# Sixteen-bit masks in a weight conversion, one table product for kv, token maxima for the second batch, and a re-planned start of a fused attention and two-layer kernel

## The chip, the cores and the metric

The kernel runs on one core of one Trainium2 chip. The metric is device microseconds (us) of one execution. PE is TensorE (matrix products and transposes), DVE is VectorE, ACT is ScalarE, POOL is GpSimd, SP issues most transfers. Each engine works through its own instruction queue in order.

## The reference, cut to what matters

```python
def _attn_ref(q, k, v):                    # each (8, 8, 576, 64), float32
    q_s = softmax of q over the 64 features
    k_s = softmax of k over the 576 tokens
    kv = np.einsum('bhsd,bhse->bhde', k_s, v)
    return np.einsum('bhsd,bhde->bhse', q_s, kv)

def _moe_ref(x, w_in, w_out, s, b):        # x: (4608, 512), w_in (512, 2048), w_out (2048, 512)
    r = np.maximum(x @ w_in, 0.0)
    return (s * (r * r) + b) @ w_out
```

Both softmaxes subtract the maximum and add 1e-9 to the sum. The two weights arrive as 64-bit floats; everything else is 32-bit.

## The kernel before, in words

**The main work.** The tokens are cut into blocks of 512: one block per batch (its first 512 tokens), and a ninth block made of the 64 tokens that each batch has left over. For each block the 2048 columns of `w_in` are taken in 16 chunks `f`. A step `t` = 16 * block + f has two halves. `h_parts` (L522) makes `h` with 12 products, four 128-row chunks `c` of x times three terms: every 32-bit operand is split into a rounded part and a remainder, and high-high, high-low and low-high are summed. `o_parts` (L590) makes four token tiles times three terms, 12 products more, into `acc`. Between them lie the relu, square, scale and split that give `gh` and `gl`. All products of 512 columns run at one pace, so 144 steps of 24 products are the bulk of the run.

**Attention.** Two heads make a unit `u`, two units (four heads) a pair `pr`; a batch has two pairs. Block 0 needs units 0 to 3 (tiles x0 to x3, one per chunk `c`), block 1 needs units 4 to 7. From the third batch on, `pair` (L400) is mixed into the main loop (L721) by the framework's own ordering.

**The first 16 steps** are ordered by a planner inside the kernel, `Order` (L113). Every stage of every stream is an `Op` with an engine, a guessed cost and a due number; `Order.run` repeatedly takes the op that can start first and, among those on its engine that can start within 0.1 us, the one with the lowest due number. What it chooses is the program order of PE, DVE, ACT and SP. Its streams:

- `transfers` (L635), on SP: k of units 0 and 1, weight 0, v of pair 0, q of pair 1, k of units 2 and 3, v of pair 1, the scalars s and b, weights 1 to 4. `others` (L658), on ACT's queue: q of pair 0. `reload` (L674): pairs 2 and 3, each into the buffers of an earlier pair, so k and v wait until that pair's kv is made.
- `conv_w(f)` (L182) turns the 64-bit weight chunk f (both matrices, 128 x 1024 values) into a high and a low 32-bit part: ACT L193 and L196, DVE L199 (keeps the top two bits of the high word and ORs in three bits of the low word), L203, L205, L208, ACT L213, DVE L215. Chunk 0 is done in two halves of 512, due at -2; chunk f is due at f - 2.
- `k_stream(u)` (L300): five transposes (L308), a maximum over the tokens (L311), an exponential with its sum (L316), five transposes back (L321, L322), two copies (L324, L325). The transposes use the PSUM buffer `big`, of which there is one.
- `kv_stream(pr)` (L327): 1/sum (L332, L334), 40 small products (L288), then the result scaled into the diagonal blocks of `kvf`, whose other blocks were zeroed once (L62): four instructions of 64 x 64, on DVE for pairs 0 and 1 (L348), on ACT for pairs 2 and 3 (L350).
- `q_stream(u)` (L352): maximum, subtraction, exponential, sum, reciprocal and product over the features (L361 to L375), five transposes into `big` (L379), a copy (L382), four products with `kvf` (L389), the split into x (L395, L398). The latter two use PSUM tag `acc` (two buffers) for units 0 to 3 and `big` for 4 to 7.
- `step(t)` (L555): the products, a relu on ACT (L563), and then either DVE L576, ACT L578, DVE L543, or, for t below 12 that are no multiple of 4, ACT L567, L569, L571 and DVE L573.

In `pair` the maximum over tokens is taken differently: over the token tiles on DVE (L414 to L416), two transposes (L420), one reduction (L422), two transposes that spread it (L426), a subtraction (L428), an exponential (L433), and a zeroing of the padding on POOL (L434). The sum comes from a 65th column of ones beside v.

Of the kernel before, what the change touches and what calls it, by code (L numbers as in the profile page):

```python
# [11 lines left out]
U32 = mybir.dt.uint32  # L12
AF = mybir.ActivationFunctionType
# [12 lines left out]
def attention_moe(ctx: ExitStack, tc: tile.TileContext, q, k, v, w_in, w_out, s, b, out):  # L26
# [34 lines left out]
    for t in kvfs:  # L61
        nc.gpsimd.memset(t, 0.0)  # L62
# [42 lines left out]
    class Op:  # L105

        def __init__(self, eng, cost, due, needs=(), take=(), free=(), gives=(), kb=0):
            self.eng, self.cost, self.due, self.kb = eng, cost, due, kb  # L110
            self.needs, self.take, self.free, self.gives = needs, take, free, gives

    class Order:  # L113
# [3 lines left out]
        NEAR, HOP, TRIP, RATE = 0.1, 0.15, 1.8, 0.3  # L117
# [22 lines left out]
        def run(self, streams):  # L140
            heads = [[next(g), 0.0, g] for g in streams]
            while heads:
# [9 lines left out]
                heads[i][1] = end = self.at[eng] = t + o.cost  # L152
# [29 lines left out]
    def conv_w(f, some):  # L182

        due = f - AHEAD
# [12 lines left out]
        yield Op("DVE", 1.13 * two, due)  # L197
# [69 lines left out]
    def loads(pr):  # L267
        tiles[pr] = raws[0]
        main, left = sources(pr)
        for which in range(2):  # L270
# [7 lines left out]
        nc.sync.dma_start(vt[0:LEFT, :, NQ, 0:D], left(v, 0, 4))  # L278

# [11 lines left out]


# [33 lines left out]

    def kv_stream(pr):  # L327
        us = (2 * pr, 2 * pr + 1)
        due = DUE[us[1]]
        yield Op("DVE", 0.2, due, needs=[f"z{u}" for u in us])  # L330
        z = zs.pop(pr)
        nc.vector.tensor_scalar(z, z, 1e-9, None, op0=ALU.add)  # L332
        zr = small.tile([P, 2], F32, name=f"zr_{pr}", tag="zr")
        nc.vector.reciprocal(zr, z)  # L334
# [4 lines left out]
        if pr < NP // 2:  # L339
            yield Op("DVE", 0.5, due, free=["sm"], gives=[f"kvf{pr}"])  # L340
        else:
            yield Op("ACT", 1.28, due, free=["sm"], gives=[f"kvf{pr}"])
        for i in range(2):
            for h in range(2):
                r = slice(h * D, (h + 1) * D)
                o, a, c = kvfs[pr % 2][r, i, h, :], kv[r, i], zr[r, i:i + 1]
                if pr < NP // 2:
                    nc.vector.tensor_scalar(o, a, c, None, op0=ALU.mult)  # L348
                else:
                    nc.scalar.activation(o, a, AF.Copy, scale=c)  # L350

    def q_stream(u):  # L352
        pr, i = divmod(u, 2)
        bb, hp = divmod(u, NP)
        due, (tag, bufs) = DUE[u], wide(u)
# [24 lines left out]
        yield Op("ACT", 0.53, due, free=["big"])  # L380
# [18 lines left out]

    def pair(pr):  # L400
# [9 lines left out]

        m2 = work.tile([P, 4, 2, D], F32, name=f"m2_{pr}", tag="m2")
        m1 = work.tile([P, 4, D], F32, name=f"m1_{pr}", tag="m1")
        with held():
            nc.vector.tensor_tensor(out=m2, in0=kt[:, :, 0:2], in1=kt[:, :, 2:4], op=ALU.max)  # L414
        nc.vector.tensor_tensor(out=m1, in0=m2[:, :, 0], in1=m2[:, :, 1], op=ALU.max)
        nc.vector.tensor_tensor(out=m1[0:LEFT], in0=m1[0:LEFT], in1=kt[0:LEFT, :, NQ], op=ALU.max)  # L416
        yield
        kT = sm("kT")
        for i in range(2):
            nc.tensor.transpose(kT[:, i * P:(i + 1) * P], m1[:, 2 * i:2 * i + 2].rearrange("p h d -> p (h d)"), ident)  # L420
        km = small.tile([P, 2], F32, name=f"km_{pr}", tag="km")
        nc.vector.tensor_reduce(out=km, in_=kT[:, 0:2 * P].rearrange("p (u s) -> p u s", u=2), axis=AX.X, op=ALU.max)  # L422
        yield
        mb = sm("mb")
        for i in range(2):
            nc.tensor.transpose(mb[:, i * P:(i + 1) * P], km[:, i:i + 1].to_broadcast([P, P]), ident)  # L426
        for i in range(2):
            nc.vector.tensor_tensor(  # L428
                out=kts[i], in0=kts[i],
                in1=mb[:, i * P:(i + 1) * P].rearrange("p (h d) -> p h d", h=2).unsqueeze(2).to_broadcast([P, 2, NT, D]),  # L430
                op=ALU.subtract,
            )
            nc.scalar.activation(kts[i], kts[i], AF.Exp)  # L433
            nc.gpsimd.memset(kts[i][LEFT:P, :, NQ], 0.0)  # L434
            yield
# [15 lines left out]
        z = small.tile([P, 2], F32, name=f"z_{pr}", tag="z")  # L451
        nc.vector.tensor_scalar(z, kv[:, :, D], 1e-9, None, op0=ALU.add)
        zr = small.tile([P, 2], F32, name=f"zr_{pr}", tag="zr")
        nc.vector.reciprocal(zr, z)
        kvf = kvfs[pr % 2]
        for i in range(2):
            for h in range(2):
                r = slice(h * D, (h + 1) * D)
                nc.vector.tensor_scalar(kvf[r, i, h, :], kv[r, i, 0:D], zr[r, i:i + 1], None, op0=ALU.mult)
# [95 lines left out]
    def step(t):  # L555
# [8 lines left out]
        if t < 12 and t % 4:  # L564
# [199 lines left out]
```

## Time and profile before

| | |
|---|---|
| median of 3 runs | 907.41 us (907.05 to 909.71) |
| profiled execution, its own time | 907.33 us |
| its span, first to last instruction | 905.5 us |
| PE busy / DVE busy / ACT busy / POOL busy over the span | 879.9 / 471.9 / 358.9 / 83.4 us |
| moved from memory and back | 46.14 MB read, 10.49 MB written |

Busy times say little by themselves: the first 150 us and the rest have different limits. The views used are the busy time by stretches, the waits, the instructions in order of time, the chain that ended last, and the groups by source line.

### The profile page before, as it was taken

The numbers are of one execution on the slowest core, as the hardware profiler recorded it, in microseconds if no ns is written. First come the engines' busy times: TensorE is split into PE (matmuls) and PEld (weight loads), VectorE is DVE, ScalarE is ACT, GpSimd is POOL, SyncE is SP. The second block draws the span as 40 slices with busy tenths as digits, with TensorE's granted clock in tenths as the row PEclk, the third lists the DMA queues.
The fourth block names the chain that finished last, engine by engine and source line by source line (L and its number), as shares of the span: only waits on it lengthen the run. The fifth ranks groups of instructions, "written<-read, shape, count | busy, mean of one in ns | idle before, by whom it ended". The sixth has DMA issues, their size and how long they took to land.

```text
span 905.5 us, 11459 instructions
## 1 busy us (share of the span) xinstructions
PE 879.9 (97%) x4560; PEld 724.0 (80%) x4560; DVE 471.9 (52%) x742; ACT 358.9 (40%) x578; POOL 83.4 (9%) x105
## 2 busy tenths in 40 slices
PE   4699999999999999999999999999999999999997
PEld 3477788888888888888888888888888888888885
DVE  7999994555454536363555446553636332223222
ACT  4899963333333423333333334333323322222222
POOL 1000000211020202020021002020202110000000
PEclk9999999999999999999999999999999999999999
DMA  9975231303130302221130313030300110001001
GB/s 230 311 258 176 92 82 47 79 4 79 50 80 4 79 4 78 48 58 27 47 79 4 82 47 79 4 79 20 105 7 1 50 47 0 1 1 47 0 1 47
DMA packets 82340, 57.36 MB, mean 63 GB/s; under 512 B 52976, under 2 KB 77552, under 8 KB 82160
## 3 DMA queue, kind: packets, MB, share of 16 engines
q1 hardware_dynamic: 81168, 55.52, 21.2%
q10 hardware_dynamic: 1120, 1.11, 0.4%
q8 instruction: 36, 0.59, 0.3%
q14 instruction: 16, 0.13, 0.0%
HBM read 46.14 MB, written 10.49 MB: 63 GB/s over the span
## 4 chain that ended last, share of the span: by engine, by line
PE 87%; DVE 7%; DMA 3%; ACT 1%; issue 1%; SPq 0%; ACTq 0%; DVEq 0%
PE acc L604 40%; PE h L530 40%; PE xp L493 2%; PE kv L288 2%; DMA st<-in_moe_w_in_dram 2%; PE qT L476 1%; DVE low L208 1%; DMA q<-in_q_dram 1%; DVE low L199 1%; DVE w L215 1%; DVE st L203 1%; DVE qm L361 1%; DVE km L311 0%; ACT w L213 0%; DVE st L205 0%
## 5 line engine op out<-in xcount | busy, mean ns | idle before, releaser
L530 PE MATMUL h<-x,w 128*128 128x512 f32 x1728 | 428.0, 394 | 4.2 <-ACT r L563 1.8
L530 PEld LDWEIGHTS h<-x,w 128*128 128x128 f32 x1728 | 321.8, 188 | 72.8 <-ACT r L563 2.8
L604 PE MATMUL acc<-w,gh 128*128 128x512 f32 x1152 | 340.3, 392 | 0.0
L604 PEld LDWEIGHTS acc<-w,gh 128*128 128x128 f32 x1152 | 215.0, 188 | 44.0 <-ACT o L617 0.4
L551 DVE SCALAR_TENSOR_TENSOR r<-r,sb 128x512 f32<-128x512 f32 x128 | 101.4, 792 | 274.2 <-ACT r L550 274.1
L604 PE MATMUL acc<-w,gl 128*128 128x512 f32 x576 | 207.8, 393 | 0.0
L550 ACT ACTIVATE r<-h 128x512 f32<-128x512 f32 x128 | 76.4, 597 | 295.9 <-PE h L530 288.8
L543 DVE SCALAR_TENSOR_TENSOR gl<-r,sb,gh 128x512 fp32r<-128x512 f32 x135 | 105.2, 780 | 86.7 <-ACT gh L552 84.7
L552 ACT ACTIVATE gh<-r,sb 128x512 fp32r<-128x512 f32 x128 | 92.7, 724 | 93.6 <-DVE r L551 93.0
L604 PEld LDWEIGHTS acc<-w,gl 128*128 128x128 f32 x576 | 108.1, 188 | 23.8 <-DVE gl L573 1.1
L443 POOL TENSOR_TENSOR q<-q,qm 128x640 f32<-128x640 f32 x24 | 30.3, 1262 | 433.4 <-DVE qm L442 432.1
L470 POOL TENSOR_TENSOR qe<-qe,qr 128x640 f32<-128x640 f32 x24 | 30.3, 1262 | 56.1 <-DVE qr L469 50.9
L433 ACT ACTIVATE k<-k 128x640 f32<-128x640 f32 x24 | 17.6, 737 | 22.4 <-DVE k L428 22.4
L466 DVE TENSOR_REDUCE qs<-qe 128x10 f32<-128x640 f32 x24 | 19.6, 818 | 12.7 <-ACT qe L445 12.7
L96 DVE TENSOR_TENSOR x<-xp,x 128x512 fp32r<-128x512 f32 x24 | 16.6, 691 | 16.9 <-ACT x L95 16.9
L445 ACT ACTIVATE qe<-q 128x640 f32<-128x640 f32 x24 | 17.6, 732 | 19.2 <-POOL q L443 19.2
L96 DVE TENSOR_TENSOR ql<-qT,qh 128x576 fp32r<-128x576 f32 x24 | 18.2, 758 | 12.0 <-ACT qh L95 12.0
L95 ACT CAST qh<-qT 128x576 fp32r<-128x576 f32 x24 | 15.4, 642 | 19.6 <-PE qT L476 19.6
L493 PE MATMUL xp<-qh,kvhl 128*128 128x256 f32 (+1 forms) x96 | 23.1, 297 | 0.0
L288 PEld LDWEIGHTS kv<-v,k 128*64 128x64 f32 x600 | 19.2, 140 | 4.2 <-issue 2.4
L428 DVE TENSOR_TENSOR k<-k,mb 128x640 f32<-128x640 f32 x24 | 18.6, 815 | 6.2 <-PE mb L426 6.2
L288 PE MATMUL kv<-v,k 128*64 128x65 f32 (+1 forms) x600 | 21.2, 226 | 0.0
(102 smaller groups left out, 543.6 us busy)
## 6 DMA issues: line engine op xcount, KB each, us to landing
st<-in_moe_w_in_dram SPq DMA_DIRECT2D x16, 512.0 KB, 8.5
st<-in_moe_w_out_dram SPq DMA_DIRECT2D x16, 512.0 KB, 8.9
out_dram<-o SPq DMA_DIRECT2D x16, 512.0 KB, 2.6
q<-in_q_dram SPq DMA_DIRECT2D x14, 512.0 KB, 4.8
v<-in_v_dram SPq DMA_DIRECT2D x48, 128.0 KB, 4.9
k<-in_k_dram SPq DMA_DIRECT2D x12, 512.0 KB, 4.8
k<-in_k_dram SPq DMA_DIRECT2D x12, 128.0 KB, 4.7
v<-in_v_dram SPq DMA_DIRECT2D x3, 512.0 KB, 4.2
```

What stands on the lines that cost most here:

```text
L96: return eng_l.tensor_tensor(out=l, in0=src, in1=h.bitcast(F32), op=ALU.subtract)
L288: nc.tensor.matmul(kv[h * D:(h + 1) * D, i], kt[:, i, h, n], vt[:, 2 * i + h, n], start=(n == 0), stop=(n == NT - 1))
L443: nc.gpsimd.tensor_tensor(out=qt, in0=qt, in1=bc(qm, [P, 2, NT, D]), op=ALU.subtract)
L466: nc.vector.tensor_reduce(out=qs, in_=qe, axis=AX.X, op=ALU.add)
L470: nc.gpsimd.tensor_tensor(out=qe, in0=qe, in1=bc(qr, [P, NT, 2, D]), op=ALU.mult)
L493: nc.tensor.matmul(t[:, 0:src.stop - src.start], lhs, rhs[:, src], start=(j == 0), stop=(j == len(terms) - 1))
L530: nc.tensor.matmul(hp_, w[:, j, c, :], x[:, c, :], start=(c == 0 and i == 0), stop=(c == NP - 1 and i == 2))
L543: gls.append(nc.vector.scalar_tensor_tensor(out=gl, in0=r, scalar=b_col, in1=gh.bitcast(F32), op0=ALU.add, op1=ALU.subtract))
L550: nc.scalar.activation(r, hp_, AF.Relu)
L551: nc.vector.scalar_tensor_tensor(out=r, in0=r, scalar=s_col, in1=r, op0=ALU.mult, op1=ALU.mult)
L552: nc.scalar.activation(gh, r, AF.Identity, bias=b_col)
L604: last = nc.tensor.matmul(a, g[:, js], w_, start=(f == 0 and i == 0), stop=(f == NFC - 1 and i == 2)).ins
```

## The change

In the conversion L199 becomes a one-operand mask on 16-bit words: the top halves of the high words, ANDed with 0xC000, are written over the top halves of `low`. Every scaling of kv becomes one product with a 128 x 4 table `zr` that holds 1/sum on its own block and zero on the other, so `kvf` needs no zeroing; the table costs one small product with a constant mask `own`. Pairs 2 and 3 take k as `pair` does (`k_pair`, `kv_second`), with v laid out with the 65th column. Steps 13, 14 and 15 take the form with three ACT instructions. The due numbers are given for k, q and kv apart; weight 0 becomes due at 9 and weight f at f - 1; the planner counts PE twice as slow before 18 us and has other transfer constants. qT takes the tag that xp has. SP's order is k0, k1, weight 0, v0, k2, v1, q1, k3, weights 1 to 4, and s and b move to ACT's queue, ahead of the exponential's table load.

```diff
-    AHEAD = 2
+    AHEAD = 1
...
-    DUE = (-9, -9, -8, -8, 3.5, 4.5, 8, 10)
+    DUE_K = (-24, 9, -27, -9, 4, 0, 10, 0)
+    DUE_Q = (-16, -12, -24, -12, 7.5, 11.5, -16, 30)
+    DUE_V = (-30, -30, -15, 14)
+    DUE_W = 9
...
-    for t in kvfs:
-        nc.gpsimd.memset(t, 0.0)
+    own = const.tile([P, 2, 2], F32, name="own")
+    nc.gpsimd.memset(own, 0.0)
+    for h in range(2):
+        nc.gpsimd.memset(own[h * D:(h + 1) * D, :, h], 1.0)
...
-        NEAR, HOP, TRIP, RATE = 0.1, 0.15, 1.8, 0.3
+        NEAR, HOP, TRIP, RATE = 0.1, 0.15, 2.8, 0.33
+        COLD = 18
...
-        due = f - AHEAD
+        due = f - AHEAD if f else DUE_W
...
-        nc.vector.scalar_tensor_tensor(
-            out=low, in0=hi, scalar=0xC0000000, in1=low, op0=ALU.bitwise_and, op1=ALU.bitwise_or
+        nc.vector.tensor_scalar(
+            low.bitcast(U16).rearrange("p n (e t) -> p n e t", t=2)[:, :, :, 1], stg.bitcast(U16)[:, :, :, 3],
+            0xC000, None, op0=ALU.bitwise_and
         )
...
+    def scales(pr, z, src):
+
+        nc.vector.tensor_scalar(z, src, 1e-9, None, op0=ALU.add)
+        nc.vector.reciprocal(z, z)
+        zr = small.tile([P, 2, 2], F32, name=f"zr_{pr}", tag="zr")
+        nc.vector.tensor_tensor(out=zr, in0=own, in1=z.unsqueeze(2).to_broadcast([P, 2, 2]), op=ALU.mult)
+        return zr
+
+    def blocks(pr, kv, zr):
+        kvf = kvfs[pr % 2]
+        shape = [P, 2, 2, D]
+        nc.vector.tensor_tensor(
+            out=kvf, in0=kv.unsqueeze(2).to_broadcast(shape), in1=zr.unsqueeze(3).to_broadcast(shape), op=ALU.mult
+        )
+        return kvf
...
+    def k_pair(pr):
...
+        yield Op("DVE", 1.13, due, needs=[f"k{u} there" for u in us])
...
+        k_max_2(kt, m2)
+        yield Op("DVE", 0.9, due)
+        k_max_1(kt, m2, m1)
+        yield Op("PE", 0.25, due, take=["sm"])
+        kT = sm("kT")
+        k_turn(m1, kT)
+        yield Op("DVE", 0.35, due, free=["sm"])
+        k_top(kT, km)
+        yield Op("PE", 0.25, due, take=["sm"])
+        mb = spread(km, sm("mb"))
+        for i, u in enumerate(us):
+            yield Op("DVE", 0.73, due, free=["sm"] if i else (), gives=[f"k{u} less"])
+            k_less(kts[i], mb, i)
+        for i, u in enumerate(us):
+            yield Op("ACT", 0.63, due, gives=[f"k{u}"])
+            k_exp(kts[i])
...
-        yield Op("PE", 0.6, due, take=["big", "qf"], free=["qe"])
-        qT = ps.tile([P, 1024], F32, name=f"qT_{u}", tag="big")
+        yield Op("PE", 0.6, due, take=[tag, "qf"], free=["qe"])
+        qT = ps.tile([P, 2, 512], F32, name=f"qT_{u}", tag=tag, bufs=bufs).rearrange("p a b -> p (a b)")
...
-        if t < 12 and t % 4:
+        if t % 4:
...
-        for i in range(2):
-            yield from some_k(0, i)
+        yield from some_k(0, 0)
+        yield from some_k(0, 1)
         yield from fetch(0)
         yield from whole(0, 2, "v")
+        yield from some_k(1, 0)
+        yield from whole(1, 2, "v")
         yield from whole(1, 1, "q")
-        for i in range(2):
-            yield from some_k(1, i)
-        yield from whole(1, 2, "v")
-        nc.sync.dma_start(s_col, s.partition_broadcast(P))
-        nc.sync.dma_start(b_col, b.partition_broadcast(P))
+        yield from some_k(1, 1)
         for f in range(1, NFE):
             yield from fetch(f)
...
         load_heads(0, 1, nc.scalar)
+        nc.scalar.dma_start(s_col, s.partition_broadcast(P))
+        nc.scalar.dma_start(b_col, b.partition_broadcast(P))
...
-        due = DUE[2 * pr] - 2
-        return [
-            (x for i in range(2) for x in some_k(pr, i, due, [f"kv{p}"])),
-            whole(pr, 1, "q", due, [f"qe{2 * p}", f"qe{2 * p + 1}"]), whole(pr, 2, "v", due, [f"kv{p}"]),
-        ]
+        due = DUE_K[2 * pr] - 2
+
+        def v_():
+            yield Op("SP", 3.2, due, needs=[f"kv{p}"], gives=[f"v{pr} there"], kb=864)
+            load_v(pr)
+
+        return whole(pr, 0, "k", due, [f"kv{p}"]), whole(pr, 1, "q", due, [f"qe{2 * p}", f"qe{2 * p + 1}"]), v_()
```

`k_max_2` to `k_exp` are the lines of `pair` (L414 to L434) made into functions. `kv_second` makes kv with the 65th column and then calls `scales` and `blocks`, as `kv_stream` and `pair` now do. `load_v` is the v part of `loads` (L267), with its two memsets at pair 2 instead of pair 4: five transfers, where `load_heads` has two. k of pairs 2 and 3 comes by `load_heads` in two transfers, where `load_k` of two units has six.

## Rows read from the trace of the kernel before

**Rows 1.** By stretches: us; busy of PE, PEld, DVE, ACT, POOL; PEclk, DMA share, GB/s.

```profile
6.22:18.00 11.78, 6.93 (x41) 5.74 (x43) 11.61 (x22) 7.30 (x15) 0.00 (x0) 1.00 1.16 291
18.00:39.10 21.10, 14.65 (x130) 10.15 (x127) 20.75 (x41) 14.89 (x28) 0.00 (x0) 1.00 0.92 259
...
46.34:113.00 66.66, 65.56 (x336) 51.60 (x334) 66.22 (x88) 62.25 (x94) 0.00 (x0) 1.00 0.51 173
113.00:148.00 35.00, 35.00 (x192) 28.64 (x193) 25.42 (x35) 20.07 (x33) 0.93 (x2) 1.00 0.22 54
148.00:837.00 689.00, 689.00 (x3576) 572.30 (x3575) 323.72 (x529) 230.02 (x376) 79.56 (x88) 1.00 0.16 44
```

**Rows 2.** The waits of PE from 46.34 to 148 us, all there are.

```profile
PE kn L321 <- ACT qf L382: 0.5, 1, 0.5
PE qT L379 <- DVE x L398: 0.4, 1, 0.4
```

**Rows 3.** Instructions in order of time on PE: start, length, idle before and its releaser.

```profile
42.27 4.46 PE L530 MATMUL h<-x,w 128*128 128x512 f32 x12 [1.83 <-ACT r L563]
...
87.98 0.71 PE L308 MATMUL kT<-ident,k 128*128 128x128 f32 x5
88.45 0.71 PE L604 MATMUL acc<-w,gh 128*128 128x512 f32 x2
```

**Rows 4.** The same on ACT, before the relu of step 0.

```profile
39.42 1.16 ACT L193 ACTIVATE low<-st 128x1024 int32<-128x1024 uint32 x1 [2.22 <-DMA st<-in_moe_w_out_dram]
...
41.64 0.58 ACT L563 ACTIVATE r<-h 128x512 f32<-128x512 f32 x1
```

**Rows 5.** The same on SP's queue: the second half of weight 3.

```profile
33.59 0.60 SPq L179 DMA_DIRECT2D st<-in_moe_w_out_dram  x1
```

**Rows 6.** Two shorter stretches around the start of step 1, columns as in rows 1.

```profile
36.00:42.00 6.00, 2.85 (x13) 1.56 (x11) 5.05 (x7) 3.74 (x6) 0.00 (x0) 1.00 0.96 315
42.00:46.50 4.50, 4.23 (x12) 3.40 (x13) 4.25 (x5) 4.48 (x6) 0.00 (x0) 0.62 1.07 391
```

**Rows 7.** The chain that ended last: start, length, what; one step's h.

```profile
142.49 2.72 PE h L530 x12
```

**Rows 8.** Groups by line and shape on DVE, 0 to 148 us: busy us, mean ns | idle before.

```profile
L199 DVE SCALAR_TENSOR_TENSOR low<-st,low 128x1024 uint32<-128x1024 uint32 x15 | 18.2, 1216 | 0.0
L208 DVE CUSTOM_DVE_ANT_0 low<-st,low 128x2048 uint16<-128x2048 uint16 x15 | 18.2, 1214 | 0.0
L203 DVE TENSOR_SCALAR st<-st 128x1024 f32<-128x1024 f32 x15 | 10.4, 690 | 0.0
...
L573 DVE TENSOR_TENSOR gl<-r,gh 128x512 fp32r<-128x512 f32 x9 | 6.2, 686 | 0.2 <-ACT gh L571 0.2
L311 DVE TENSOR_REDUCE km<-kT 128x1 f32<-128x576 f32 x8 | 6.0, 752 | 0.1
L543 DVE SCALAR_TENSOR_TENSOR gl<-r,sb,gh 128x512 fp32r<-128x512 f32 x8 | 6.0, 746 | 2.4 <-ACT gh L578 1.6 <-ACT gh L552 0.8
...
L348 DVE TENSOR_SCALAR kvf<-kv,zr 64x64 f32<-64x64 f32 x8 | 2.3, 283 | 0.1
```

**Rows 9.** The same on DVE from 150 to 830 us: the parts of `pair`.

```profile
L428 DVE TENSOR_TENSOR k<-k,mb 128x640 f32<-128x640 f32 x24 | 18.6, 815 | 6.2 <-PE mb L426 6.2
...
L414 DVE TENSOR_TENSOR m<-k 128x512 f32<-128x512 f32 x11 | 7.6, 689 | 2.8 <-PE xp L493 2.8
...
L415 DVE TENSOR_TENSOR m<-m 128x256 f32<-128x256 f32 x12 | 5.0, 415 | 0.0
```

**Rows 10.** The same on ACT, 0 to 148 us.

```profile
L569 ACT ACTIVATE r<-r,sb 128x512 f32<-128x512 f32 x9 | 7.4, 822 | 0.1
...
L350 ACT ACTIVATE kvf<-kv,zr 64x64 f32<-64x64 f32 x8 | 2.5, 309 | 0.1
```

**Rows 11.** In order of time on DVE: the last instruction of the last conversion.

```profile
133.38 1.23 DVE L215 TENSOR_TENSOR w<-low,w 128x1024 fp32r<-128x1024 f32 x1 [0.45 <-ACT w L213]
```

**Rows 12.** The same on PE: the rest of the h of step 15.

```profile
136.88 2.20 PE L530 MATMUL h<-x,w 128*128 128x512 f32 x9
```

More of the change, by code (lines that the diff above doesn't have):

```diff
@@ L151, in run @@
                 o, ready, g = heads[i]
-                heads[i][1] = end = self.at[eng] = t + o.cost
+                heads[i][1] = end = self.at[eng] = t + o.cost * (2 if eng == "PE" and t < self.COLD else 1)
                 if o.kb:
@@ L278, in loads @@
         nc.sync.dma_start(vt[0:LEFT, :, NQ, 0:D], left(v, 0, 4))
+    def loads(pr):
+        tiles[pr] = raws[0]
+        for which in range(2):
+            load_heads(pr, which, nc.sync)
+        load_v(pr)
     def bc(t, shape):
@@ L301, in k_stream @@
         pr, i = divmod(u, 2)
-        due, (tag, bufs) = DUE[u], wide(u)
-        yield Op("PE", 0.6, due, needs=[f"k{u} there"] + [f"x{NP - 1}"] * (u >= NP), take=["big", "ke"])
+        due, (tag, bufs) = DUE_K[u], wide(u)
+        yield Op("PE", 0.6, due, needs=[f"k{u} there"], take=["big", "ke"])
         kt = by_tile(tiles[pr][0])
@@ L338, in kv_stream @@
         heads(kv, kt.rearrange("p u n h d -> p u h n d"), vt)
[L339 to L342, printed above, removed]
-        for i in range(2):
[L344 to L350, printed above, removed]
+        yield Op("DVE", 0.4, due, free=["sm"], gives=[f"kvf{pr}"])
+        blocks(pr, kv, zr)
     def q_stream(u):
@@ L354, in q_stream @@
         bb, hp = divmod(u, NP)
-        due, (tag, bufs) = DUE[u], wide(u)
+        due, (tag, bufs) = DUE_Q[u], wide(u)
         before = [f"kv{NP // 2 - 1}"] + [f"qe{u}" for u in range(NP - 2, NP)]
@@ L408, in sm @@
             return ps.tile([P, 512], F32, name=f"{n}_{pr}", tag="sm", bufs=1)
-        m2 = work.tile([P, 4, 2, D], F32, name=f"m2_{pr}", tag="m2")
-        m1 = work.tile([P, 4, D], F32, name=f"m1_{pr}", tag="m1")
+        m2, m1, km = k_tiles(pr)
         with held():
-            nc.vector.tensor_tensor(out=m2, in0=kt[:, :, 0:2], in1=kt[:, :, 2:4], op=ALU.max)
-        nc.vector.tensor_tensor(out=m1, in0=m2[:, :, 0], in1=m2[:, :, 1], op=ALU.max)
-        nc.vector.tensor_tensor(out=m1[0:LEFT], in0=m1[0:LEFT], in1=kt[0:LEFT, :, NQ], op=ALU.max)
+            k_max_2(kt, m2)
+        k_max_1(kt, m2, m1)
         yield
         kT = sm("kT")
+        k_turn(m1, kT)
+        k_top(kT, km)
+        yield
+        mb = spread(km, sm("mb"))
         for i in range(2):
[L420 to L424, printed above, removed]
-        for i in range(2):
[L426 to L434, printed above, removed]
+            k_less(kts[i], mb, i)
+            k_exp(kts[i])
             yield
@@ L450, in pair @@
         heads(kv, kt.rearrange("p (u h) n d -> p u h n d", u=2), vt)
[L451 to L459, printed above, removed]
+        kvf = blocks(pr, kv[:, :, 0:D], scales(pr, small.tile([P, 2], F32, name=f"z_{pr}", tag="z"), kv[:, :, D]))
         kvhl = work.tile([P, 2, 2, 2 * D], F32R, name=f"kvhl_{pr}", tag="m2")
@@ L650, in some_k @@
     def some_k(pr, i, due=0, needs=()):
-        yield Op("SP", 1.9, due, needs=needs, gives=[f"k{2 * pr + i} there"], kb=320)
+        yield Op("SP", 1.9, due, needs=needs, gives=[f"k{2 * pr + i} there"], kb=480)
         load_k(pr, i)
     def whole(pr, which, n, due=0, needs=()):
-        yield Op("SP", 1.3, due, needs=needs, gives=[f"{n}{pr} there"], kb=576)
+        gives = [f"k{2 * pr} there", f"k{2 * pr + 1} there"] if which == 0 else [f"{n}{pr} there"]
+        yield Op("SP", 1.3, due, needs=needs, gives=gives, kb=576)
         load_heads(pr, which, nc.sync)
```

72 lines of the change are left out of this document (56 added, 16 removed).

## The prediction

> **What bounds the kernel now.** I read the busy time by stretches first, because an average over 905.5 us hides that there are two regimes. From 148 to 837 us PE is busy 689.00 of 689.00 us [rows 1]: only PE's own work counts there, and nothing that DVE, ACT or POOL gain is worth anything. From 46.34 us on PE is already nearly full (65.56 of 66.66, then 35.00 of 35.00), and the list of its waits over those 102 us holds two entries, 0.9 us together [rows 2]. What can be won is therefore either PE work or the time before 46.34.
>
> In that front the instructions in order of time show that step 1 starts its products at 42.27, after 1.83 us of waiting for the relu of step 0 [rows 3]. The relu stood in ACT's queue behind L193, which waited 2.22 us for the second half of weight 3, and behind L196 [rows 4]. That half was issued only at 33.59 [rows 5], because SP had the six k loads and two v loads of pair 2 in front of it. Step 1 then ran at a reduced clock: a granted 0.62 on average, 4.23 us of PE for 12 products that take 2.72 later [rows 6, 7].
>
> Behind all that stands DVE: busy 11.61 of 11.78 us and 20.75 of 21.10 us up to 39.10, the end of the fourth x tile (x3, the last that step 0 needs) [rows 1]. It stays at 66.22 of 66.66 up to 113. So the front is DVE's, and from 46 on DVE and PE are full side by side; only after 113 has DVE 9.6 us to spare (35.00 less 25.42).
>
> **The change, part by part.** I count against the profiled execution's own 907.33 us (span 905.5 and 1.83 around it); the median, 907.41, is 0.08 higher, which is nothing.
>
> *PE work.* Units 4 to 7 lose five transposes to kT and five back each. Five cost 0.47 us from start to start (87.98 to 88.45) [rows 3], so 8 x 0.47 = 3.8 us go. `k_pair` adds four per pair, 8 x 0.094 = 0.75. Net 3.0 us off PE, and since PE has no idle time behind 46 us, they come off the end.
>
> *The mask.* Fifteen whole conversions and one in two halves lose L199 at 1.216 us. The trace has no one-operand DVE instruction on 16-bit words with gaps between them. Cheap end: L208 does 2048 16-bit words in 1.214, so 1024 in 0.61. Dear end: no faster than L199, 1.216. I take L203's 0.690, the nearest: one tensor, one constant, 1024 elements with gaps between them [rows 8]. 16 x (1.216 - 0.690) = 8.4 us off DVE.
>
> *kv scaling.* Four L348 of 0.283 (1.13 us) become one product of 128 x 256 and a small one. The first reads PSUM, which L415 does not; I take L415's 0.415, with L311's 0.752 (more columns, from PSUM) as the dear end; the small one at most one L348, 0.283, at least nothing. About 0.45 off per pair [rows 8, 9], 0.9 for pairs 0 and 1. Pairs 2 and 3 had this on ACT (8 x 0.309 = 2.5 us [rows 10]); it moves to DVE, plus 0.7 each. The twelve later pairs gain on a DVE that PE covers: nothing.
>
> *k of pairs 2 and 3.* Per pair DVE gains L414's 0.689, two maxima like L415 (0.83), a reduction of 256 columns (below L311's 0.752; I take 0.42) and two L428 (1.63): 3.6 us, for two L311 (1.5) that go: plus 2.1 each [rows 8, 9]. With the scaling, 2 x 2.8 = 5.6 us onto DVE.
>
> *Steps 13 to 15.* Two instructions like L543 become one L573: 3 x (1.49 - 0.69) = 2.4 off DVE. ACT gets two more in each, at most 3 x 2 x 0.822 = 4.9 us, and gives up the 2.5 above, eight copies out of PSUM and four accumulator reads [rows 8, 10]: about level, so not counted; its cover is that DVE and PE are fuller.
>
> DVE in all: -8.4 - 0.9 + 5.6 - 2.4 = **-6.1 us**.
>
> *Queues.* s and b move past SP's queue to ACT's, two issues ahead of a table load, long before the first exponential; nothing. The six k issues of a later pair become two and the two of v five, behind two POOL memsets: one issue fewer per pair on SP, and whatever stands behind them, the weights 2 to 4, still waits for pair 0's kv. q of pair 1 now stands behind k of unit 2 and v of pair 1; its first reader is a DVE that has weight 0 and units 0 and 1 to work on meanwhile. The transposes of q leave the single `big` buffer, so k of units 2 and 3 no longer queues behind q of 0 and 1: this is what lets kv of pair 1 come early.
>
> *The front.* DVE did 32.4 us of work between 6.22 and 39.10 [rows 1]. Of it x3 did not need: weight 1's conversion (L199, L208 and L215 at 1.22, L203 and, taken like it, L205 at 0.690: 5.0 us [rows 8, 11]), weight 0's second half (2.5), one L199 of weight 2 (1.2) and a maximum of unit 4 (taken as L311, 0.75). 9.4 in all; with 0.9 for kv and 0.3 for the mask, 21.8 us remain, so x3 cannot come before 28.0. The other end is 39.10, nothing gained. Step 1 also needs weight 0's rest and all of weight 1, now 2.2 + 4.5 us: 34.7 at the earliest. A round through PE and ACT after that is not free, so I take 36 for the start of step 1, against 42.27: **6.3 us** (between 0 and 7.6). If the clock does not fall again, 4.23 - 2.72 = **1.5 us** [rows 6, 7].
>
> Here row and rule can differ. By the rows the clock fell after a stretch in which PE was busy 2.85 of 6.00 us [rows 6]; a front that is 6 us shorter has fewer such holes, so I count the 1.5 us. The Trainium skill (TensorE: Matmul & The Clock Gate, Part 4: PE-mode transpose) holds that transposes do not count as work for the clock gate; the front is still mostly transposes, so by that the clock could fall all the same, and the sum below would end at 901.7 instead of 900.2. No row here separates the two.
>
> *Late landings.* At 42.27 PE lost 1.83 us to one [rows 3]. The transfers still take 0.92 of their time or more up to 39 us [rows 1], pair 2's loads still go ahead of weights, and q of pair 1 is issued later. I charge two such waits, 3.7 us (none at best).
>
> PE's side: 3.0 + 6.3 + 1.5 - 3.7 = **7.1 us**, hence **900.2 us**.
>
> *DVE's room.* 7.1 us earlier needs DVE to be that much earlier too. It has 6.1 less to do; its spare time lies mostly behind the last conversion, whose result was ready at 134.6 (133.38 + 1.23) and used at 136.88 [rows 11, 12], 2.3 us of slack. So DVE caps the gain at 6.1 + 2.3 = 8.4, and the 7.1 are just under it.
>
> **The rivals.**
>
> *The front stays where it is.* Step 1 waits for something else at about 42: a weight behind pair 2's loads, or unit 1, whose k is now due at 9. For it: the transfers are full either way. Against it: DVE, not a landing, held x3. Then only PE's 3.0 remain: 904.3 (903 to 906).
>
> *The mask is no faster* (1.216 stays). DVE is then 8.4 - 6.1 = 2.3 us heavier than before, its cap is -2.3 + 2.3 = 0, and 907.3 comes out. For it: no such access in the trace. Against it: L203.
>
> *Slower: the mask is dearer than what it replaces*, because half words are written between others. The cap falls by 16 us for each us of the mask: from about 1.39 us on, the run is over 2.7 us slower (2.7 us, 0.3%, is about what a measurement of this kernel can tell from no change). At twice L199, 2.43, DVE would carry 19 us more: 927. For it: both sides have gaps. Against it: L208 writes 16-bit words at 0.59 ns each.
>
> **How the numbers follow.** Forecast 0.66 (896.5 to 904.6), better still 0.03, front stays 0.15, mask no faster 0.08, mask dearer 0.08. Faster by over 0.3% (below 904.6): 0.66 + 0.03 + about half of 0.15 = 0.77. Within: the other half and the mask that is no faster, 0.15. Slower: 0.08. The range runs from 896.5 (no late landing, and DVE's cap loosened to 10.8 by a mask at 0.61 and a free small product) to 906.5 (an unmoved front with one more late landing of 1.83, rounded up); it leaves out the last two rivals and the best.
>
> **What would show it.** The mask at about 0.69 us; PE's first product of step 1 near 36 us; granted clock 1.00 from there on; PE's waits after that still around 1 us; DVE's busy time up to the handover to the main loop some 6 us lower; PE busy from then on without a gap. Wrong would be: step 1 at 40 us or later, new waits of PE for `w` (DVE L215) between steps 3 and 15, a mask above 1.2 us, or idle PE behind step 16.

## The result, and the profile after

The changed kernel takes 900.11 us (median of 4 runs, 899.77 to 900.48) against 907.95 us for the kernel before, run beside it: a ratio of 0.9911, 95% interval 0.9894 to 0.9929. Its profiled execution took 900.48 us with a span of 898.7, so the two profiled spans differ by 6.8 us. 900.2 was forecast. The sum holds, but not all of its terms do: two gains came out smaller, and a loss that was charged against them came to about a quarter of its size.

By stretches (us; busy of PE, PEld, DVE, ACT, POOL; granted clock, DMA share, GB/s), the changed kernel:

```profile
36.00:42.00 6.00, 4.43 (x12) 3.06 (x13) 6.00 (x9) 5.81 (x9) 0.00 (x0) 0.80 1.01 231
42.00:46.50 4.50, 4.50 (x19) 3.60 (x19) 4.50 (x7) 3.81 (x5) 0.00 (x0) 0.88 0.86 273
46.00:113.00 67.00, 65.78 (x360) 52.62 (x359) 66.16 (x96) 60.61 (x80) 0.96 (x4) 1.00 0.58 186
113.00:148.00 35.00, 34.80 (x157) 27.91 (x156) 23.50 (x38) 18.90 (x31) 0.00 (x0) 1.00 0.17 53
148.00:837.00 689.00, 689.00 (x3577) 572.49 (x3576) 315.38 (x500) 229.71 (x375) 79.67 (x88) 1.00 0.16 42
...
0.00:141.60 141.60, 123.78 (x677) 98.06 (x678) 123.15 (x195) 110.95 (x164) 3.94 (x22) 0.99 0.62 184
```

The picture is that of [rows 1]: PE without a gap from 148 to 837 us, PE and DVE both nearly full from 46 to 113. The last row ends 0.2 us after the 12 products of one step begin (141.37); they began at 147.76 before. DVE had been busy 130.04 us up to 148 then and is busy 123.15 us now: 6.9 less, where 6.1 was forecast.

The waits of PE behind step 1, all of them:

```profile
PE h L600 <- ACT r L633: 0.7, 2, 0.5
PE acc L674 <- DVE gl L643: 0.5, 2, 0.3
PE qT L433 <- DVE x L452: 0.2, 1, 0.2
```

1.4 us, against 0.9 in [rows 2]. In order of time on all three engines, the start of step 1 (rows of other instructions between them left out), answering [rows 3, 4]:

```profile
20.18 1.55 DVE L415 TENSOR_REDUCE qm<-raw 128x10 f32<-128x640 f32 x2 [0.87 <-DMA raw<-in_q_dram]
...
30.43 1.17 ACT L202 ACTIVATE low<-st 128x1024 int32<-128x1024 uint32 x1
31.63 1.22 ACT L205 ACTIVATE st<-st 128x1024 f32<-128x1024 f32 x1
...
31.37 0.81 DVE L415 TENSOR_REDUCE qm<-q 128x10 f32<-128x640 f32 x1
...
32.69 0.83 DVE L417 TENSOR_TENSOR q<-q,qm 128x640 f32<-128x640 f32 x1
...
35.76 0.75 DVE L208 TENSOR_SCALAR low<-st 128x1024 uint16<-128x1024 uint16 x1
36.40 0.68 DVE L452 TENSOR_TENSOR x<-xp,x 128x512 fp32r<-128x512 f32 x1
36.99 0.69 DVE L213 TENSOR_SCALAR st<-st 128x1024 f32<-128x1024 f32 x1
37.59 1.23 DVE L225 TENSOR_TENSOR w<-low,w 128x1024 fp32r<-128x1024 f32 x1
38.07 0.68 ACT L633 ACTIVATE r<-h 128x512 f32<-128x512 f32 x1
38.80 4.61 PE L600 MATMUL h<-x,w 128*128 128x512 f32 x12 [0.94 <-ACT r L633]
43.24 0.62 PE L674 MATMUL acc<-w,gh 128*128 128x512 f32 x2
```

Step 1 starts at 38.80, 3.5 us earlier than before. The fourth x tile (L452 at 36.40) is finished at 37.08, 2.0 earlier. The first product follows the relu (L633, ended at 38.75), and the last instruction of weight 1 (L225) ended with it, at 38.82. Up to there DVE worked almost without a break: its list of waits from 20 to 128 us, over 100 us, is

```profile
DVE qm L415 <- DMA raw<-in_q_dram: 0.9, 1, 0.9
DVE low L208 <- issue: 0.2, 1, 0.2
DVE w L225 <- ACT w L223: 0.2, 1, 0.2
```

and from its first instruction (6.32) to 38.82 the first of these, for q of pair 1, is the only one. Ahead of the end of weight 1 DVE did work that step 1 does not need: L415 and L417 of unit 4, L208 and L213 of weight 2, 2.7 us from start to start. ACT did such work too (2.4 us on weight 2, 1.2 on weight 3, 0.8 on unit 4), but DVE did not wait for it. The clock fell again: 0.80 and 0.88 granted in the first two stretches, and the 12 products took 4.44 us (38.80 to 43.24), much as before (their row says 4.61, against 4.46 in [rows 3]).

Groups by line and shape on DVE, 0 to 148 us (busy us, mean ns), answering [rows 8, 9]:

```profile
L208 DVE TENSOR_SCALAR low<-st 128x1024 uint16<-128x1024 uint16 x15 | 11.2, 763 | 0.2 <-issue 0.2
...
L480 DVE TENSOR_TENSOR k<-k,mb 128x640 f32<-128x640 f32 x4 | 3.3, 817 | 0.0
...
L316 DVE TENSOR_TENSOR kvf<-kv,zr 128x256 f32<-128x256 f32 x4 | 1.7, 418 | 0.0
...
L464 DVE TENSOR_TENSOR m<-m 128x256 f32<-128x256 f32 x3 | 1.3, 430 | 0.0
...
L472 DVE TENSOR_REDUCE km<-kT 128x2 f32<-128x256 f32 x2 | 0.8, 422 | 0.0
...
L310 DVE TENSOR_TENSOR zr<-own,z 128x4 f32<-128x4 f32 x4 | 0.7, 162 | 0.2
```

L208 is the new mask: 763 ns, where 690 was taken. The product for kv (418 ns), the reduction (422) and the subtraction (817) came out at the values that were taken for them.

### The profile page after: what moved, and what is told of

It is laid out like the page before. It is cut to its first block, busy times and chain, and to the rows that moved or that the text cites. A ratio compares the mean times of both kernels' runs of the same rounds, so it can differ in the third digit from the quotient of the medians.

```text
span 898.7 us, 11364 instructions
## 1 busy us (share of the span) xinstructions
PE 876.0 (97%) x4528; PEld 721.8 (80%) x4528; DVE 459.5 (51%) x723; ACT 357.4 (40%) x564; POOL 83.6 (9%) x110
## 4 chain that ended last, share of the span: by engine, by line
PE 89%; DVE 4%; ACT 3%; DMA 2%; SPq 1%; issue 1%; ACTq 0%; DVEq 0%
PE h L600 41%; PE acc L674 41%; PE xp L563 2%; PE kv L301 2%; PE qT L546 1%; ACT low L202 1%; DMA raw<-in_q_dram 1%; DVE w L225 1%; ACT st L205 1%; DMA k<-in_k_dram 1%; PE xp L443 0%; DMA q<-in_q_dram 0%; ACT r L633 0%; DVE low L218 0%; DVE st L215 0%
## 5 line engine op out<-in xcount | busy, mean ns | idle before, releaser
L613 DVE SCALAR_TENSOR_TENSOR gl<-r,sb,gh 128x512 fp32r<-128x512 f32 x132 | 102.6, 777 | 84.6 <-ACT gh L622 84.2
L487 ACT ACTIVATE k<-k 128x640 f32<-128x640 f32 x28 | 20.4, 736 | 20.1 <-DVE k L480 20.1
L480 DVE TENSOR_TENSOR k<-k,mb 128x640 f32<-128x640 f32 x28 | 21.9, 816 | 7.3 <-PE mb L476 7.3
```

What stands on the lines that cost most here:

```text
L480: nc.vector.tensor_tensor(out=kt, in0=kt, in1=mb[:, i * P:(i + 1) * P].rearrange("p (h d) -> p h d", h=2).unsqueeze(2).to_broadcast([P, 2, ...
L613: gls.append(nc.vector.scalar_tensor_tensor(out=gl, in0=r, scalar=b_col, in1=gh.bitcast(F32), op0=ALU.add, op1=ALU.subtract))
```

## The experiments

All of them start from the changed kernel, save the third. Medians are of 4 to 11 runs each. The half intervals of the ratios come to 0.8 to 1.6 us, so differences of a microsecond or so are not told apart. The runs were made in three sessions, and beside them the kernel before took 908.35 to 908.62 us, 0.4 to 0.7 more than beside the changed kernel. Below, medians are subtracted as they are; by the ratios the mask, the transposes, the scalings and the steps come to 6.8, 2.5, 2.5 and 2.2 us instead of 7.1, 2.9, 2.9 and 2.8.

**The mask undone, in the new order.**

```diff
-        nc.vector.tensor_scalar(
-            low.bitcast(U16).rearrange(...)[:, :, :, 1], stg.bitcast(U16)[:, :, :, 3], 0xC000, None, op0=ALU.bitwise_and
+        nc.vector.scalar_tensor_tensor(
+            out=low, in0=hi, scalar=0xC0000000, in1=low, op0=ALU.bitwise_and, op1=ALU.bitwise_or
```

> The changed kernel with the two-operand mask of before put back; every engine's order is that of the changed kernel, instruction for instruction. DVE gets 15 x (1.216 - 0.763) + 2 x (0.662 - 0.450) = 7.2 us more. Theory 'DVE caps the gain': the last conversion then ends some 7 us later than 127.1, of which about 3 us are slack before step 15 needs it, so the run is 4 us slower, 904 to 905, and PE shows new waits for products of DVE. Rival 'PE alone': behind step 1 PE is full whatever DVE does, only the four masks ahead of step 1 count (2 x 0.2 + 2 x 0.45 = 1.3 us): 901.4.

Measured: 907.21 us, ratio 0.9986 (0.9978 to 0.9995). Waits of PE from 46 to 148 us:

```profile
PE acc L674 <- DVE gl L643: 4.0, 6, 1.7
PE h L600 <- DVE w L225: 1.1, 1, 1.1
PE h L600 <- ACT r L633: 0.8, 2, 0.6
```

The run is 7.1 us above the changed kernel, and the mask's own saving is 15 x (1.216 - 0.763) + 2 x 0.21 = 7.2. So DVE's time goes into the end nearly one for one, and PE waits for `gl` and `w`: in the new order DVE, which in the changed kernel idles for only 0.4 us between step 1 and the end of the last conversion (127.14), holds PE up to there. In this profile the clock fell early (below), which adds to the 7.1; the seven executions with the mean granted clock of the changed kernel's profiled one, 0.997, took 906.70 to 907.60 us against its 900.48, so the mask alone is worth 6.2 to 7.1.

**The transposes put back** (32 more in `k_turn` for pairs 2 and 3, written where the useful ones write).

```diff
-        k_turn(m1, kT)
+        k_turn(m1, kT, 9)
...
-    def k_turn(m1, kT):
-        for i in range(2):
+    def k_turn(m1, kT, n=1):
+        for i in (0, 1) * n:
```

> The changed kernel with the two transposes of the token maxima of pairs 2 and 3 repeated nine times (32 transposes more, same result; all orders otherwise unchanged): the number of PE transposes of before is put back, and nothing else. Theory 'PE work comes off the end whole': 32 x 0.094 = 3.0 us slower, 903.1. Rival 'DVE caps the gain, PE has room': 0 to 1 us slower.

Measured: 903.01 us, ratio 0.9938 (0.9924 to 0.9951), 2.9 us more than the changed kernel. PE's own work comes off the end whole, within the interval.

**The mask alone, in the kernel before** (the same edit as in the first, the other way).

> The kernel before with the new mask and nothing else, all orders unchanged. DVE has 7.2 us less to do. Theory 'PE was full from 46 us on': only what the mask gives ahead of step 1 counts (two halves and two whole ones, 1.3 us): 906.6. Rival 'the mask is the change': most of the 7.2 us: 901.

Measured: 906.47 us, ratio 0.9976 (0.9966 to 0.9986), a gain of 2.0 us over the 908.48 of the kernel before in the same session.

```profile
30.00:46.00 16.00, 13.19 (x85) 10.02 (x86) 13.38 (x24) 12.56 (x19) 0.00 (x0) 0.82 0.89 277
46.00:113.00 67.00, 66.57 (x345) 52.85 (x344) 65.12 (x91) 64.60 (x97) 0.00 (x0) 1.00 0.54 178
```

The same edit that is worth 6.2 to 7.1 us in the new order is worth 2.0 in the old: there DVE has idle time in the front (13.38 of 16.00) and PE is full behind it (66.57 of 67.00). What a faster DVE gives is decided by the order. The 2.0 us agree with the expected number, but the reason that was expected, masks ahead of step 1, is not what the trace shows: in the profiled execution (906.64 us, against 907.33 for that of the kernel before) step 1 began at 44.17, later than the 42.27 of before.

**All the new instructions in the old order** (the planner's numbers, the buffer of qT and the order of transfers as before).

```diff
-    AHEAD = 1
+    AHEAD = 2
...
-    DUE_K = (-24, 9, -27, -9, 4, 0, 10, 0)
-    DUE_Q = (-16, -12, -24, -12, 7.5, 11.5, -16, 30)
-    DUE_V = (-30, -30, -15, 14)
-    DUE_W = 9
+    DUE_K = DUE_Q = (-9, -9, -8, -8, 3.5, 4.5, 8, 10)
+    DUE_V = DUE_K[1::2]
+    DUE_W = -2
...
```

> All the new instructions (mask, table product, token maxima, steps 13 to 15) with the planner's numbers, due numbers, SP's order and qT's buffer of before. Theory 'the parts and the order add up': PE's 3.0 us and the mask's 2.0 us come off the 907.4, 902.4, and step 1 stays at 41 to 42 us. If the new order is worth nothing by itself: 900 to 900.5. If the parts need the new order: 905 or more.

Measured: 905.25 us, ratio 0.9966 (0.9954 to 0.9979): 3.4 us better than the kernel before. The new order gives the rest, some 5 us.

**q of pair 1 first.**

```diff
+        yield from whole(1, 1, "q")
         yield from some_k(1, 0)
+        yield from some_k(1, 1)
         yield from whole(1, 2, "v")
-        yield from whole(1, 1, "q")
-        yield from some_k(1, 1)
```

> The changed kernel with q of pair 1 ahead of k of unit 2 and v of pair 1 on SP again, as before (the planner then orders the rest anew). In the changed kernel DVE waited 0.87 us for this q, and x2 and x3 come out of its chain. Theory 'the late q holds x3': q lands some 4 us earlier, step 1 starts 1 to 2 us before 38.80, the run takes 898.5 to 899.5. Rival 'kv of pair 1 and ACT's queue hold x3': step 1 no earlier, 900 to 901.

Measured: 925.95 us, ratio 1.0189 (1.0175 to 1.0203). It does not isolate the late q: k of unit 3 also moved, ahead of v, and the planner ordered all that follows anew, and two transfers of leftover tokens then sat in SP's queue for 7.45 us in front of the weights.

```profile
40.04 7.45 SPq L244 DMA_DIRECT2D xleft<-xleft  x2
47.53 0.46 SPq L186 DMA_DIRECT2D st<-in_moe_w_in_dram  x1
```

From 42 to 46.5 us DVE and ACT did nothing at all. A small change of the planner's input is no small change of the order. The new order also takes unit 2 before unit 1, and `keep_left` (L238), which gathers leftover tokens by twos, then sends out those of unit 2 in place of unit 0's: this order gives a time, but not the reference's output.

**q of pair 1 on ACT's queue**, with the rest of the order left as it is.

```diff
-        load_heads(pr, which, nc.sync)
+        if (pr, which) != (1, 1): load_heads(pr, which, nc.sync)
...
-        nc.scalar.dma_start(b_col, b.partition_broadcast(P))
+        nc.scalar.dma_start(b_col, b.partition_broadcast(P)); load_heads(1, 1, nc.scalar)
```

> The changed kernel with q of pair 1 issued on ACT's queue right behind q of pair 0, s and b (about 3 to 4 us) instead of by SP at 13.6; all other orders unchanged. It takes the transfers' time from k of unit 1, weight 0 and k of unit 2, which land up to 2 us later. Theory 'the late q holds x3': DVE's 0.87 us of idle before it goes and step 1 starts about 0.9 us before 38.80: 899.2. Rival 'something else holds x3' (ACT's conversions in the way of x2 and x3): no gain, 900 to 901.

Measured: 900.72 us, ratio 0.9913 (0.9898 to 0.9929); step 1 at 38.91. DVE's wait of 0.87 us for that q is gone, but three others stand ahead of it now that the changed kernel does not have, 0.9 us together:

```profile
15.14 0.46 DVE L208 TENSOR_SCALAR low<-st 128x512 uint16<-128x512 uint16 x1 [0.48 <-ACT low L202]
16.56 0.17 DVE L307 TENSOR_SCALAR z<-z 128x2 f32<-128x2 f32 x1 [0.28 <-ACT ke L344]
19.04 0.76 DVE L339 TENSOR_REDUCE km<-kT 128x1 f32<-128x576 f32 x1 [0.18 <-PE kT L336]
```

DVE came to q of pair 1 at 20.31, where it had been 20.18. So this run moved the wait and did not remove it; what the late landing costs is seen below, where holes on PE are filled.

**The four scalings of kv put back**, same order.

```diff
...
-        nc.vector.tensor_tensor(
-            out=kvf, in0=kv.unsqueeze(2).to_broadcast(shape), in1=zr.unsqueeze(3).to_broadcast(shape), op=ALU.mult
-        )
+        for i in range(2):
+            for h in range(2):
+                r = slice(h * D, (h + 1) * D)
+                nc.vector.tensor_scalar(kvf[r, i, h, :], kv[r, i], zr[r, i:i + 1], None, op0=ALU.mult)
```

> The changed kernel with kv scaled by four DVE instructions of 64 x 64 again, in all pairs; the order of the first 16 steps is unchanged. DVE gets about 1.2 - 0.42 - 0.08 = 0.7 us more per pair, 2.5 to 2.8 us in the first 16 steps. Theory 'DVE binds behind step 1, us for us' (as with the old mask): 902.3. Rival 'slack takes it': 900.1 to 900.6.

Measured: 903.0 us, ratio 0.9939 (0.9927 to 0.9952): 2.9 us, for 4 x (1.13 - 0.418 - 0.162) = 2.2 us of DVE. That agrees with one for one, within the interval.

**Steps 13 to 15 put back.**

```diff
-        if t % 4:
+        if t < 12 and t % 4:
```

> The changed kernel with steps 13, 14 and 15 in the form with two DVE products again (the planner's order differs only around them). DVE gets 2.4 us more, but behind 128 us, where it idles some 9 us before the main loop. Theory 'DVE binds up to its last conversion and not behind it': 900.1, within 0.5. Rival 'DVE us for us everywhere': 902.5.

Measured: 902.92 us, ratio 0.9935 (0.9922 to 0.9947), 2.8 us, for 2.4 us of DVE. DVE's idle time of 9.2 us behind the last conversion did not cover them: PE waited 0.7 us for the relu of a step there. But 1.1 us was lost ahead of step 1 (39.92), where the order is that of the changed kernel, so that is not the edit: the clock fell early in this execution (0.50 from 22 to 24 us), and DVE waited 0.99 us for an x tile. The record has the mean granted clock of every execution: the five times are 901.46 at 0.999 and 902.90 to 903.18 at 0.995 and 0.996. Compared at like clocks with executions without the edit (899.77 to 900.29 at 0.999 and 1.0 in the changed kernel; 901.39 to 901.63 at 0.995 and 0.996 in two kernels below, with the same early fall), the edit is worth 1.2 to 1.8 us, less than its 2.4 us of DVE.

**PE's holes in front of step 1 filled**, with eight products in one kernel and 20 transposes in another, into a buffer that step 0 overwrites.

```diff
             hp_ = next(parts)
+            if t == 0 and c > 1:
+                for _ in range(4):           # the other kernel: 10 transposes of ident
+                    nc.tensor.matmul(acc[0, 0][:, 0], wi[0][:, 0, 0, :], x_tile(0)[0][:, 0, :], start=True, stop=True)
```

> The changed kernel, with eight more products of 512 columns on PE (four behind the third x chunk of step 0, four behind the fourth), written to a buffer that step 0 overwrites later: they fill holes in which PE sat idle in the changed kernel (0.44 us before the last chunk, 0.94 us before step 1) and use 8 x 0.227 = 1.8 us at full clock. Theory A (the clock falls because PE had holes in front of step 1): the granted clock stays at 1.00 from 36 to 46 us, step 1's 12 products take 3.0 us instead of 4.6, step 1 starts at 38.8 to 39.3. If PE's time in the front counts for the end, 898.5 to 899.5; if DVE, which is full up to 113 us, sets the end all the same, 899.8 to 900.8 and PE's waits behind 46 us grow from 1.4 to about 3 us. Rival B (the fall has another cause): granted 0.50 again somewhere from 38 to 44 us, step 1's products 4.6 us, 900 to 901.5.

> The same holes filled with 20 transposes of a constant (10 and 10, 0.094 each, 1.9 us) in the place of products. By what the rows of the kernels so far show, the clock fell after stretches in which PE had been idle, with products and transposes alike in them: then this run goes as the one filled with products, within 0.4 us. If transposes do not count as work, the clock falls in this run and not in that one: granted 0.50 somewhere from 38 to 44 us and 4.6 us for step 1's products here against 1.00 and 3.0 us there. The Trainium skill (TensorE: Matmul & The Clock Gate, Part 4: PE-mode transpose) holds that they do not count.

Measured: 900.73 us with products (ratio 0.9919, 0.9905 to 0.9932) and 901.05 with transposes (0.9919, 0.9905 to 0.9933). With products the clock did not fall, and step 1's products, which began at 37.69, took 3.02 us. By stretches:

```profile
36.00:42.00 6.00, 5.87 (x26) 4.49 (x26) 6.00 (x9) 5.71 (x8) 0.00 (x0) 1.00 0.96 196
...
37.69:140.14 102.45, 100.63 (x509) 79.27 (x509) 92.05 (x136) 83.70 (x114) 0.98 (x4) 1.00 0.48 146
```

From the start of step 1 to the same products of the later step it is 102.45 us here and 102.57 in the changed kernel (38.80 to 141.37). The 1.4 us won on PE were lost again by 140 us. What remains is the earlier start, 1.1 us, and it arose at 19 us, ahead of the filled holes, with 1.00 granted in both: here q of pair 1 had landed when DVE came to it,

```profile
19.16 1.54 DVE L415 TENSOR_REDUCE qm<-raw 128x10 f32<-128x640 f32 x2
```

and from there to step 1 it is 18.5 us, against 18.6 in the changed kernel. So the late landing was on the path, for about 1 us. The span of this execution is 1.3 us shorter (897.4), but 3.0 us of its time lie outside the span, against 1.8 in the changed kernel, and the medians of the spans are alike (898.2 in five executions, 898.3 in four): no gain in time is shown. With transposes the clock fell earlier, ahead of the filled holes (the same columns):

```profile
18.00:20.00 2.00, 0.42 (x4) 0.42 (x5) 1.20 (x2) 1.42 (x3) 0.45 (x2) 1.00 1.30 235
...
22.00:24.00 2.00, 1.24 (x4) 0.99 (x4) 2.00 (x4) 0.74 (x1) 0.00 (x0) 0.50 1.05 374
24.00:28.00 4.00, 3.46 (x14) 2.55 (x13) 2.87 (x10) 2.60 (x6) 0.00 (x0) 0.50 1.10 346
36.00:42.00 6.00, 6.00 (x36) 4.95 (x35) 5.83 (x8) 5.92 (x9) 0.00 (x0) 1.00 0.96 218
```

So the pair cannot say whether transposes count as work for the clock; that stays open.

**DVE relieved further: q of units 4 to 7 on POOL**, once with the planner's knowledge and a new order, once in the order as it stands.

```diff
-        nc.vector.tensor_tensor(out=qt, in0=qt, ..., op=ALU.subtract)
+        (nc.gpsimd if u >= NP else nc.vector).tensor_tensor(out=qt, in0=qt, ..., op=ALU.subtract)
-        nc.vector.tensor_tensor(out=qe, in0=qe, ..., op=ALU.mult)
+        (nc.gpsimd if u >= NP else nc.vector).tensor_tensor(out=qe, in0=qe, ..., op=ALU.mult)
```

> The changed kernel with the subtraction and the product of q of units 4 to 7 on POOL instead of DVE (8 x about 0.82 us off DVE, 8 x about 1.27 on POOL as in the main loop); the planner knows it and orders the rest anew. Theory (DVE is the bound up to 113 us, and after that only PE's own 1.4 us of waits and the front are left to win): DVE has 6.5 us less, one subtraction of 0.83 goes from in front of the last instruction of weight 1, so step 1 starts at about 38.0 instead of 38.8; waits behind it 0.5 to 1.0 us; 898.4 to 899.8. Rival (a new order by the planner brings stalls, as q of pair 1 ahead of k did, or POOL's longer way of each unit is waited for): 901 to 906, with a wait of PE for xp or qT behind POOL.

> The same eight instructions on POOL, but with the planner's order of everything else left as in the changed kernel. Theory: 898.4 to 899.8, step 1 at about 38.0. Rival (DVE's sums behind them now wait for POOL in a queue that was ordered for the shorter times, and hold up the conversions): DVE idle 2 us or more between 46 and 113 in front of the sums of qe, 900 to 902.

Measured: 911.03 us with the new order (ratio 1.0032, 1.0020 to 1.0043), PE busy only 59.12 of 67.00 us from 46 to 113. The rival was right in that the new order brought stalls, but not in which: PE waited only 0.3 us for POOL, and longest for `gh` and `gl` of the steps.

```profile
PE acc L674 <- ACT gh L641: 2.9, 1, 2.9
PE acc L674 <- DVE gl L643: 2.6, 4, 1.0
```

This order takes unit 6 before unit 5, so here too `keep_left` sends out wrong leftover tokens. In the order as it stands 900.00 us (0.9912, 0.9899 to 0.9926): no gain and no loss. Three of DVE's groups in that kernel from 0 to 148 us (busy us, mean ns), and then two places on POOL and DVE in order of time, the first ahead of step 1:

```profile
L213 DVE TENSOR_SCALAR st<-st 128x1024 f32<-128x1024 f32 x15 | 12.8, 857 | 0.0
L215 DVE TENSOR_SCALAR st<-st 128x1024 uint32<-128x1024 uint32 x15 | 11.3, 757 | 0.0
...
L646 DVE SCALAR_TENSOR_TENSOR r<-r,sb 128x512 f32<-128x512 f32 x4 | 4.0, 996 | 0.0
```

```profile
33.18 1.58 POOL L417 TENSOR_TENSOR q<-q,qm 128x640 f32<-128x640 f32 x1 [14.70 <-DVE qm L415]
33.68 1.63 DVE L215 TENSOR_SCALAR st<-st 128x1024 uint32<-128x1024 uint32 x1
...
113.38 2.17 POOL L417 TENSOR_TENSOR q<-q,qm 128x640 f32<-128x640 f32 x1 [3.22 <-DVE qm L415]
...
114.34 1.76 DVE L646 SCALAR_TENSOR_TENSOR r<-r,sb 128x512 f32<-128x512 f32 x1
```

Eight instructions of 0.82 us (6.5 us) left DVE, but L213 went from 696 to 857 ns, L215 from 699 to 757 and L646 from 754 to 996: 2.4 + 0.9 + 1.0 = 4.3 us came back. Ahead of step 1 (40.02) one L215 took 1.63 us instead of 0.70, so more came back there than the 0.83 that had left. No version here is shown to beat the changed kernel.

## Why the prediction was right, and where it was not

**PE work, 3.0: right.** The second experiment gives 2.9 (2.5 by the ratios) for the same count of transposes.

**The mask, 8.4: mis-sized.** The nearest row, L203, has 32-bit elements; 16-bit ones with gaps on both sides took 763 ns, not 690. It is 7.2 us, well inside the bounds, and neither of the rivals that rest on the mask occurred.

**kv and k: right.** 0.418 and 0.162 came out, against 0.415 and at most 0.283 taken. For k of pairs 2 and 3, 0.689 + 0.430 + 0.418 + 0.422 + 2 x 0.817 = 3.6, as forecast. DVE's sum came to -6.9 instead of -6.1, although the mask fell short by 1.2; the two counts do not end at the same DVE instruction. Of the 2 us between them 0.75 is a `gl` of step 16, which is done at 147.42, inside the count before, and at 142.72, outside the count after; the rest is not placed.

**The front, 6.3: the step that failed.** It measured 3.5. The prediction took 34.7 as the earliest start and added 1.3 for a round through PE and ACT. That was a bound with only the needed work in it. It looked at the right engine: DVE's queue set the pace up to step 1. But the planner fills every free moment of an engine with whatever can start, and so put 2.7 us of other work into that queue ahead of the end of weight 1, and 0.9 us went in the wait for q of pair 1. 34.7, 2.7 and 0.9 make 38.3; DVE's first instruction came 0.1 later than was taken, needed work and small gaps took 0.4 more than was counted, and weight 1 ended at 38.82. The round through PE and ACT ended at the same time and added nothing. Taking 0.83 us off DVE there brought step 1 no earlier (40.02), because an L215 beside POOL took 0.9 us longer and because the clock had fallen early in that run (0.50 from 22 to 24 us), for which DVE waited 0.99 us.

**The clock, 1.5: mis-sized.** In the profiled execution it fell again, although the front was shorter. In others of the same kernel it did not, or not for as long: their mean granted clocks are 1.0, 1.0 and 0.999, against 0.997 in the profiled one, while none of 40 executions of the kernel before in the later sessions is above 0.999 and only two reach it. So falls are fewer or shorter in the changed kernel (whether by the shorter front is not shown), but the three took only 0.2 to 0.7 us less than the profiled one. And where the clock did not fall, step 1's 1.4 us were gone by 140 us, because DVE, not PE, sets the pace behind step 1. The Trainium skill (TensorE: Matmul & The Clock Gate, Part 4: PE-mode transpose) was given as the reason for which it could fall all the same. The fall agrees with that, but in the changed kernel nine products of 512 columns and eight for xp stood between 30 and 38 us just before it, beside five transposes, so no run here shows that transposes are the cause.

**Late landings, -3.7: mis-sized.** Weights 1 to 5 were issued ahead of pair 2's k and v (its q went ahead of weights 3 to 5), and no wait for a weight is left. One late landing, q of pair 1, held DVE for 0.87 us, and step 1 with it for about 1 us; that is inside the front's 3.5 above.

Together: 3.0 + 3.5 for the front and -0.5 for PE's waits give 6.0 of the 6.8 us between the spans; the rest has no row of its own. The forecast came out because the front's 2.8 and most of the clock's 1.5, which were missing, are nearly the 3.7 that were charged and, beyond the front, did not occur. It was the right total from partly wrong terms, and that is luck.

**DVE's room, 8.4: the part that mattered most.** With the mask at its measured size this cap is 8.4 - 1.2 = 7.2, and that is near where the result stands (6.8 between the spans, 7.8 between the medians). Put back, the mask and the scalings each cost about what they are worth on DVE (6.2 to 7.1 and 2.9 us for 7.2 and 2.2), the steps somewhat less (1.2 to 1.8 for 2.4). The prediction named PE's side as the lower one; DVE's was as low. Whether relief beyond that would give more is not shown: PE has 1.4 us of waits left behind step 1, and of the 6.5 us that went to POOL most came back as longer DVE instructions.

## What to carry to other kernels

Where two engines are full side by side, an edit has no price of its own: the same mask gave 2.0 us in one order and 6 to 7 in the other, and all new instructions together 3.4 in the old order. So forecast the edit and the order together, by the engine that is full in each stretch, and take an earliest possible start for a bound and not for an estimate when a greedy planner fills the gaps. A term that comes off an engine which is not the last to be ready (here the clock on PE) should not be counted at the size that its row shows. And a planner that is free to reorder units must know of every place where the kernel relies on their order, as `keep_left` does here.

## What the hardware showed that was not expected

**The place of the clock's fall.** Kernels with the same order on every engine up to step 1 fell at different places. In the changed kernel the granted clock was at its lower level from about 39.7 to 43 us, with the waits for x and relu before it. In the kernel with transposes filled in, and with the old mask, it was lower from about 21.6 to 28.5 us, after PE had waited 1.66 and 1.93 us near 18 us for an exponential; in the kernel filled with products 1.00 was granted from 0 to 148 us, although PE had waited 1.67 us at the same place. The two profiled executions with the early fall and no DVE work put back took 901.39 and 901.63 us, and three with a later fall or none 900.41 to 900.54. An early fall is dearer, for it delays the x tiles and with them DVE: in all five profiles of this order that have it, DVE waited 0.98 or 0.99 us for ACT's part of an x tile, and in the four with a later fall or none it did not. Other executions of those two kernels agree: at mean clocks of 0.997 to 0.999 they took 899.82 to 900.52 us, and the one more at 0.996 took 901.57. What decides where the clock falls is not shown.

**The granted clock does not tell all of PE's pace.** In the changed kernel the same four transposes took, with 1.00 granted at both places:

```profile
15.40 1.11 PE L349 MATMUL kn<-ident,ke 128*128 128x128 f32 x4 [1.02 <-ACT ke L344]
...
19.69 0.66 PE L349 MATMUL kn<-ident,ke 128*128 128x128 f32 x4
```

**POOL and DVE slow each other.** Beside POOL, L646 took 1.76 us where it takes 0.75 in the mean without POOL, and the subtractions on POOL took 1.76 us in the mean, against 1.26 in the main loop. The Trainium skill (SBUF — State Buffer, Who interferes with whom) says that a DVE instruction with two inputs in SBUF contends with a GpSimd instruction that reads SBUF, and that one-source DVE instructions in a two-port mode do too. The run agrees for L646 (+0.24 us in the mean of four) and for L213 and L215 (+0.16, +0.06), while L225, also with two inputs, stayed within 0.8% of its mean.
